# Two loads of a decode kernel cut into seven parts by partitions

## The chip, the cores and the metric

The kernel runs on one core of one Trainium2 chip. The metric is the device time of one execution in microseconds (us), the median of several runs. Five engines work side by side: PE multiplies matrices (PEld is its loading of weights), DVE and ACT work on vectors, POOL fills memory, and SP issues nearly all transfers. The transfers themselves are carried out by 16 DMA engines that the core has to itself. SBUF, the memory on the core, has 128 partitions; a load of a tile brings 128 rows from HBM, one for each partition.

## The reference

Two layers of a decode step, run twice with the same weights and caches. A layer is attention with one new token for each of 8 sequences over a cache of 4096 positions (32 query heads share 4 key and value heads), then a feed-forward network with a tanh GELU:

```python
x = x + _A_ref(_layernorm(x), A_k_cache, A_v_cache, A_wq, A_wo)
x = x + _B_ref(_layernorm(x), B_w1, B_b1, B_w2, B_b2)
x = x + _A_ref(_layernorm(x), A_k_cache, A_v_cache, A_wq, A_wo)
x = x + _B_ref(_layernorm(x), B_w1, B_b1, B_w2, B_b2)
```

with

```python
q = (x @ wq).reshape(B, Sq, Hq, Dh).transpose(0, 2, 1, 3)
p = softmax(einsum("bhqd,bhkd->bhqk", q, k) * Dh ** -0.5)
o = einsum("bhqk,bhkd->bhqd", p, v)          # then @ wo
h = gelu(x @ w1 + b1)                        # then @ w2 + b2
```

x is 8 x 1024, wq and wo are 1024 x 4096 and 4096 x 1024, w1 and w2 are 1024 x 3584 and 3584 x 1024, each cache is 8 x 4 x 4096 x 128, all in float32. Every weight and every cache is read from HBM, most of it twice, and each byte is used in one or two matmuls.

## The kernel before

All large data go through one tile, `arena` (line 58): 128 partitions of 218 units of 256 float32 (1 KB a partition). A place in it is a first unit and a number of units; 8 units (8 KB a partition, 1 MB in all) hold one piece of a cache. Three regions A, Bb and C start at units 0, 64 and 128, and a ring of four slots at 184.

`stream` (line 155) is the list of all loads in the order in which they are wanted, each with its place. `pump` (lines 158 to 163) issues from its head on SP's queue as long as the head's place is free, and `give` (line 71) frees a place behind its last use and calls `pump`. So the order of the loads is that of `stream`, and the time of an issue is set by the work that frees its place. Each issue waits on semaphores for that work, and also for the load eight places ahead of it in the queue, since eight semaphores are used in turn.

The order in `stream`: wq, then for each of the 8 sequences its K and V; K 7 and V 7, those of the last sequence, come in smaller loads, V 7 as four of 32, 16, 8 and 8 units (line 467). Then wo, w1, w2 and again wq, in loads of 8 units through the ring (lines 470 to 473). The second layer goes through the sequences backwards, and what is still in SBUF of the last two is not loaded again. At its end stand wo in two loads, w1 in two of 56 units (line 481, one for each half of the hidden units), and w2 in six of 40 to 4 units (line 482).

`values` (line 365) multiplies a piece of V with the probabilities, `expand` (line 172) a normalised row with wq or w1, and `project` (line 267) with wo or w2. `expand` goes through the loads of a half in turn (`loads`, line 165), frees them as they are used, and starts on a load when it has landed whole. Both loads of the change are read by PE alone.

The profile names w1 and w2 alike, `in_B_w_dram`, and a row of it that names L162 is an issue in `pump`.

Of the kernel before, what the change touches and what calls it, by code (L numbers as in the profile page):

```python
# [14 lines left out]
P = 128  # L15
B, D = 8, 1024
# [18 lines left out]
KB = 256  # L35
# [11 lines left out]
def decode_layers(ctx: ExitStack, tc: tile.TileContext, x, kc, vc, wq, wo, w1, b1, w2, b2, out):  # L47


    nc = tc.nc  # L50
# [7 lines left out]
    arena = const.tile([P, N_KB * KB], F32, name="arena")  # L58
# [5 lines left out]
    def is_free(at, n):  # L64
        return not any(u in used for u in range(at, at + n))

    def take(at, n, who):
        assert is_free(at, n), (who, at, n)
        used.update(dict.fromkeys(range(at, at + n), who))

    def give(at, n):
        for u in range(at, at + n):
            used.pop(u)
        pump()
# [79 lines left out]

    stream = []
    held = {}

    def pump():
        while stream and is_free(stream[0][1], stream[0][2]):
            key, at, n, src = stream.pop(0)  # L160
            take(at, n, key)
            nc.sync.dma_start(out=arena[:, at * KB:at * KB + src.shape[1]], in_=src)  # L162
            held[key] = at, n

    def loads(name):
# [137 lines left out]
    def v_keys(b):  # L303
        return [("v", b, r // NH, r % NH) for r in range(NR)]
# [124 lines left out]
    def weights(name, dram, parts, kept=0):  # L429

        for u in range(dram.shape[0]):
            a = 0
            end = dram.shape[2] - (kept if u == 1 else 0)
            for i, (at, n) in enumerate(parts[u]):
                cols = min(n * KB, end - a)
                stream.append((((name, u) if dram.shape[0] > 1 else name, i), at, n, dram[u, :, a:a + cols]))
                a += cols
            assert a == end
# [13 lines left out]
    A, C, Bb = AT_A, AT_C, AT_B  # L452
# [25 lines left out]
        cache(1, k_keys(b), kc[b], [(k_at, 8)])  # L478
        cache(1, v_keys(b), vc[b], [(v_at, 8)])
    weights("o1", wo, [[(C, SLOT), (A, SLOT)]])  # L480
    weights("i1", w1, [[(Bb, 56)], [(C, 56)]])
    weights("p1", w2, [[(A, 40), (A + 40, 28), (A + 68, 20), (A + 88, 12), (A + 100, 8), (A + 108, 4)]])

    kept = set(k_keys(7)) | set(v_keys(7)) | set(k_keys(6))
# [5 lines left out]
    open_queries()  # L490
    rsum = row_sums()
    pump()
    nc.vector.tensor_reduce(rsum, x_row, AX.X, ALU.add)  # L493
    nc.sync.dma_start(out=b2T, in_=b2)
# [111 lines left out]
```

## Time and profile before

| what | us |
|---|---|
| median of 3 runs | 871.89 (871.6 to 872.33) |
| the profiled execution | 871.66 |
| its span, first to last instruction | 869.9 |
| PE busy in it | 536.0 (62%) |
| DVE busy in it | 179.6 (21%) |
| ACT busy in it | 48.7 (6%) |

The span is what the trace covers; the 1.8 us that the execution has beyond it lie around it. The page gives busy times of each engine, the span in 40 slices, the DMA queues (q1 is SP's, q8 and q14 bring instructions, q10 is ACT's), the chain of work that ended last, and groups of instructions. In a row of the timeline the number in brackets is how long the engine sat idle before, and what ended that.

### The profile page before, as it was taken

What the parts mean: (1) busy time and instruction counts of PE and PEld (TensorE: products, weight loads), DVE (VectorE), ACT (ScalarE), POOL (GpSimd) and SP (SyncE); (2) the same over time, 40 slices, a digit from 0 to 9 for tenths busy, and PEclk for the clock granted to TensorE, in tenths of its full rate; (3) what the DMA queues carried; (4) which work ended last, traced back from release to release, by engine and by line L of the source; (5) the groups of instructions that cost most, each with busy time, mean ns of one, the idle gap of its engine ahead of it and who ended that gap; (6) DMA issues with size and microseconds to landing.
All of it is one profiled execution on the core that took longest, in us unless ns stands there. A gap on an engine that the chain in (4) does not pass through costs nothing.

```text
span 869.9 us, 9280 instructions
## 1 busy us (share of the span) xinstructions
PE 536.0 (62%) x4120; PEld 184.3 (21%) x4120; DVE 179.6 (21%) x601; ACT 48.7 (6%) x77; POOL 2.3 (0%) x13
## 2 busy tenths in 40 slices
PE   0546574655657576866666777876575555755565
PEld 0212121211212122222222122222121211222222
DVE  0001231313122232200110033332231313120011
ACT  0200000000000011000000010000000000000000
POOL 0000000000000000000000000000000000000000
PEclk9977787777777788777886798987777877778879
DMA  9999999999999999999999999999999999999997
GB/s 391 435 433 432 434 432 432 435 431 435 431 429 432 434 422 428 411 417 419 421 419 416 411 423 439 438 431 432 432 434 432 435 434 435 429 435 437 421 421 304
DMA packets 17608, 369.45 MB, mean 425 GB/s; under 512 B 2208, under 2 KB 2464, under 8 KB 4000
## 3 DMA queue, kind: packets, MB, share of 16 engines
q1 hardware_dynamic: 17424, 368.73, 99.2%
q8 instruction: 32, 0.52, 0.2%
q10 hardware_dynamic: 144, 0.13, 0.0%
q14 instruction: 8, 0.07, 0.0%
HBM read 368.72 MB, written 0.13 MB: 424 GB/s over the span
## 4 chain that ended last, share of the span: by engine, by line
DMA 75%; PE 21%; DVE 1%; another core or an unknown queue 1%; ACT 1%; issue 0%; SPq 0%; ACTq 0%; DVEq 0%
DMA arena<-in_A_v_cache_dram 28%; DMA arena<-in_A_k_cache_dram 20%; DMA arena<-in_B_w_dram 17%; PE o_ps L375 7%; PE sps L318 5%; DMA arena<-in_A_wo_dram 5%; PE acc L189 3%; DMA arena<-in_A_wq_dram 3%; DMA x_row<-in_A_x_dram 3%; PE y L283 2%; PE sps L390 1%; PE sps L353 1%; PE s_ps L318 1%; ACT arena L342 0%
## 5 line engine op out<-in xcount | busy, mean ns | idle before, releaser
L318 PE MATMUL sps<-arena 128*32 128x512 f32 x944 | 137.2, 719 | 118.4 <-DMA arena<-in_A_k_cache_dram 106.7
L375 PE MATMUL o_ps<-arena 128*32 128x512 f32 x1024 | 151.6, 732 | 10.2 <-DMA arena<-in_A_v_cache_dram 10.1
L283 PE MATMUL y<-arena,oT 128*32 128x256 f32 x960 | 79.1, 474 | 50.7 <-DMA arena<-in_A_wo_dram 31.2
L189 PE MATMUL acc<-arena,xnT 128*32 128x512 f32 (+3 forms) x640 | 78.2, 596 | 46.2 <-DMA arena<-in_B_w_dram 27.0
L318 PEld LDWEIGHTS sps<-arena 128*32 128x32 f32 x944 | 29.7, 125 | 192.9 <-DMA arena<-in_A_k_cache_dram 98.2
L383 DVE SCALAR_TENSOR_TENSOR scratch<-o_ps,misc,scratch 128x128 f32<-128x128 f32 x192 | 67.4, 351 | 6.8
L353 PE MATMUL sps<-ident,arena 128*128 128x128 f32 x128 | 31.1, 388 | 43.5 <-ACT arena L342 31.6
L283 PEld LDWEIGHTS y<-arena,oT 128*32 128x32 f32 x960 | 31.8, 129 | 94.5 <-DMA arena<-in_A_wo_dram 32.6
L375 PEld LDWEIGHTS o_ps<-arena 128*32 128x32 f32 x1024 | 33.0, 130 | 86.5 <-issue 73.8
L342 ACT ACTIVATE arena<-arena,bias 128x1024 f32<-128x1024 f32 x16 | 18.4, 1150 | 505.9 <-DVE scratch L339 505.9
L326 DVE TENSOR_SCALAR_CACHE_REDUCE arena<-sps 128x512 f32<-128x512 f32 x30 | 20.8, 692 | 124.9 <-PE sps L318 124.9
L392 DVE TENSOR_TENSOR oT<-sps,scratch 128x8 f32<-128x8 f32 x64 | 11.1, 173 | 154.4 <-PE sps L390 154.4
L189 PEld LDWEIGHTS acc<-arena,xnT 128*32 128x32 f32 x640 | 22.0, 124 | 91.4 <-DMA arena<-in_A_wq_dram 34.1
L390 PEld LDWEIGHTS sps<-misc,scratch 128*128 128x128 f32 x128 | 21.5, 211 | 63.8 <-DVE scratch L383 39.9
L381 DVE TENSOR_SCALAR scratch<-o_ps,misc 128x128 f32<-128x128 f32 x64 | 22.0, 344 | 54.7 <-PE o_ps L375 54.7
L353 PEld LDWEIGHTS sps<-ident,arena 128*128 128x128 f32 x128 | 19.7, 191 | 52.4 <-ACT arena L342 35.4
L390 PE MATMUL sps<-misc,scratch 128*128 128x8 f32 x128 | 27.4, 286 | 1.2 <-DVE scratch L383 1.2
L335 PE MATMUL sps<-scratch,misc 128*128 128x128 f32 x32 | 7.8, 326 | 18.9 <-DVE scratch L331 18.6
L295 DVE SCALAR_TENSOR_TENSOR x_row<-y,x_row 128x256 f32<-128x256 f32 x4 | 1.7, 425 | 85.0 <-PE y L283 85.0
L358 DVE COPY arena<-sps 128x512 f32<-128x512 f32 x16 | 11.1, 692 | 39.4 <-PE sps L353 39.4
L360 PE MATMUL sps<-scratch,misc 128*128 128x32 f32 x32 | 10.2, 411 | 12.5 <-DVE arena L358 12.5
L131 PE MATMUL sps<-nmean,rsum 128*128 128x64 f32 x8 | 2.1, 358 | 25.3 <-DVE rsum L493 23.6
(77 smaller groups left out, 143.2 us busy)
## 6 DMA issues: line engine op xcount, KB each, us to landing
arena<-in_B_w_dram SPq DMA_DIRECT2D x27, 1024.0 KB, 8.6
arena<-in_A_wo_dram SPq DMA_DIRECT2D x15, 1024.0 KB, 8.2
arena<-in_A_wq_dram SPq DMA_DIRECT2D x14, 1024.0 KB, 8.1
arena<-in_B_w_dram SPq DMA_DIRECT2D x2, 7168.0 KB, 45.3
arena<-in_A_k_cache_dram SPq DMA_DIRECT2D x3, 4096.0 KB, 18.2
arena<-in_A_v_cache_dram SPq DMA_DIRECT2D x3, 4096.0 KB, 24.5
arena<-in_A_v_cache_dram SPq DMA_DIRECT2D x4, 2048.0 KB, 12.0
arena<-in_A_wq_dram SPq DMA_DIRECT2D x1, 7680.0 KB, 39.9
```

The lines of the kernel that those rows point to most:

```text
L189: nc.tensor.matmul(acc[32 * j:32 * j + 32, r * P:(r + len(ts)) * P], xnT[:, kt * B:kt * B + 32], blocks[:, ts[0] - t0:ts[-1] - t0 + 1:4], ...
L283: nc.tensor.matmul(y[32 * j:32 * j + 32, 0:Q4], lhs[:, kt * B:kt * B + 32], arena[:, e:e + Q4], start=(kt == 0), stop=(kt == n_k - 1))
L318: nc.tensor.matmul(ps[32 * g:32 * g + 32, :], q[:, c:c + 32], kt[:, g * CH:(g + 1) * CH], start=(j == 0), stop=(j == HKV - 1))
L326: nc.vector.tensor_scalar(row[:, half * CH:(half + 1) * CH], ps, SCALE, None, op0=ALU.mult, op1=ALU.max, accum_out=st["mx"][:, half:half + 1])
L342: nc.scalar.activation(row, row, AF.Exp, bias=bias, scale=1.0, accum_out=ls)
L353: nc.tensor.transpose(pp[:, t * P:(t + 1) * P], row[:, c:c + P], ident)
L358: nc.vector.tensor_copy(s[:, half], src)
L375: nc.tensor.matmul(o[32 * g:32 * g + 32, :], s[:, g], v[:, g * CH:(g + 1) * CH], start=(half == 0), stop=(half == NH - 1))
L381: nc.vector.tensor_scalar(r, o[:, 0:P], sel_t[:, 0:1], None, op0=ALU.mult)
L383: nc.vector.scalar_tensor_tensor(r, o[:, t * P:(t + 1) * P], sel_t[:, t:t + 1], r, op0=ALU.mult, op1=ALU.add)
L390: nc.tensor.matmul(po[:, 0:REP], scratch[:, a:a + DH], sel_h, start=True, stop=True)
L392: nc.vector.tensor_tensor(oT_v[:, j * REP:(j + 1) * REP, b], po[:, 0:REP], scratch[:, a + j * REP:a + (j + 1) * REP], ALU.mult)
```

## The change

Two loads are picked out by their keys and kept in a set, `split`: the second of V 7 in the first layer (16 units, 2 MB, 16 KB a row) and a part of w1's second half in the second layer. For the latter the load of 56 units becomes one of 36 and one of 20 units (2.5 MB, 20 KB a row). `pump` issues a load of the set in seven parts by partitions, one behind the other on the same queue: partitions 0 to 111, then five times three partitions (112 to 126), then partition 127. Every byte still goes from the same place to the same place.

```diff
     stream = []
     held = {}
+    split = set()
+    uneven = [(0, 112)] + [(a, min(a + 3, P)) for a in range(112, P, 3)]
 
     def pump():
         while stream and is_free(stream[0][1], stream[0][2]):
             key, at, n, src = stream.pop(0)
             take(at, n, key)
-            nc.sync.dma_start(out=arena[:, at * KB:at * KB + src.shape[1]], in_=src)
+            dst = arena[:, at * KB:at * KB + src.shape[1]]
+            for a, b in uneven if key in split else ((0, P),):
+                nc.sync.dma_start(out=dst[a:b], in_=src[a:b])
             held[key] = at, n
...
-    weights("i1", w1, [[(Bb, 56)], [(C, 56)]])
+    weights("i1", w1, [[(Bb, 56)], [(C, 36), (C + 36, 20)]])
+    split.update(((0, v_keys(B - 1)[4]), (("i1", 1), 1)))
```

On SP's queue, this stood where the first layer's V 7 is loaded, followed by the first loads of wo (a row is an issue: line, target and source, partitions by float32 elements, and what it waits for; DMAHW0 to 7 are the eight semaphores of earlier loads):

```order
L162 DMA arena<-in_A_v_cache_dram 128x8192 [waits DMAHW4_49,PE_49]
L162 DMA arena<-in_A_v_cache_dram 128x4096 [waits PE_49]
L162 DMA arena<-in_A_v_cache_dram 128x2048 [waits PE_49]
L162 DMA arena<-in_A_v_cache_dram 128x2048 [waits DMAHW3_49,PE_49]
L162 DMA arena<-in_A_wo_dram 128x2048 [waits DMAHW5_49,Activation_49]
```

And this stands there now, on the same queue:

```order
L166 DMA arena<-in_A_v_cache_dram 128x8192 [waits DMAHW4_49,PE_49]
L166 DMA arena<-in_A_v_cache_dram 112x4096 [waits PE_49]
L166 DMA arena<-in_A_v_cache_dram 3x4096
L166 DMA arena<-in_A_v_cache_dram 3x4096 [waits DMAHW3_49]
L166 DMA arena<-in_A_v_cache_dram 3x4096 [waits DMAHW5_49]
L166 DMA arena<-in_A_v_cache_dram 3x4096 [waits DMAHW6_49]
L166 DMA arena<-in_A_v_cache_dram 1x4096 [waits DMAHW7_49]
L166 DMA arena<-in_A_v_cache_dram 128x2048 [waits DMAHW0_49,PE_49]
L166 DMA arena<-in_A_v_cache_dram 128x2048 [waits DMAHW1_49,PE_49]
L166 DMA arena<-in_A_wo_dram 128x2048 [waits DMAHW2_49,DVE_49]
```

The load of 128 rows of 4096 has become one of 112 rows, five of three (one of them, like the first, without a wait, is left out here) and one of a single row. The issues behind it now wait for the parts, since those stand eight places ahead of them.

On SP's queue, at the end of the second layer, this stood where w1's second half and w2 are loaded:

```order
L162 DMA arena<-in_A_wo_dram 128x16384 [waits DMAHW5_49,PE_49]
L162 DMA arena<-in_B_w_dram 128x14336 [waits DMAHW6_49,PE_49]
L162 DMA arena<-in_B_w_dram 128x14336 [waits DMAHW7_49,PE_49]
L162 DMA arena<-in_B_w_dram 128x10240 [waits DMAHW0_49,PE_49]
L162 DMA arena<-in_B_w_dram 128x7168 [waits DMAHW1_49,PE_49]
L162 DMA arena<-in_B_w_dram 128x5120 [waits PE_49]
```

And this stands there now:

```order
L166 DMA arena<-in_B_w_dram 128x14336 [waits DMAHW4_49,PE_49]
L166 DMA arena<-in_B_w_dram 128x9216 [waits DMAHW5_49,PE_49]
L166 DMA arena<-in_B_w_dram 112x5120 [waits PE_49]
L166 DMA arena<-in_B_w_dram 3x5120 x4
L166 DMA arena<-in_B_w_dram 3x5120 [waits DMAHW6_49]
L166 DMA arena<-in_B_w_dram 1x5120 [waits DMAHW7_49]
L166 DMA arena<-in_B_w_dram 128x10240 [waits DMAHW0_49,PE_49]
L166 DMA arena<-in_B_w_dram 128x7168 [waits DMAHW1_49,PE_49]
L166 DMA arena<-in_B_w_dram 128x5120 [waits DMAHW2_49,PE_49]
L166 DMA arena<-in_B_w_dram 128x3072 [waits DMAHW3_49,PE_49]
```

Where two loads of 14,336 elements a row stood there are now one of those, one of 9,216, and seven parts of 5,120; w2's first loads follow unchanged, but for what they wait for. On PE the order is the same; its matmuls on the two loads wait for the parts.

## The prediction

> **What bounds the kernel now.** I read the page first, its slices, its DMA counts and its chain.
>
> ```profile
> span 869.9 us, 9280 instructions
> ...
> DMA  9999999999999999999999999999999999999997
> GB/s 391 435 433 432 434 432 432 435 431 435 431 429 432 434 422 428 411 417 419 421 419 416 411 423 439 438 431 432 432 434 432 435 434 435 429 435 437 421 421 304
> DMA packets 17608, 369.45 MB, mean 425 GB/s; under 512 B 2208, under 2 KB 2464, under 8 KB 4000
> ...
> q1 hardware_dynamic: 17424, 368.73, 99.2%
> q8 instruction: 32, 0.52, 0.2%
> ...
> DMA 75%; PE 21%; DVE 1%; another core or an unknown queue 1%; ACT 1%; issue 0%; SPq 0%; ACTq 0%; DVEq 0%
> ```
>
> The 16 DMA engines are busy in every slice, and almost all of it is SP's queue, q1. Its count tells how a load is made: 121 issues (120 loads and the output) times 144 is 17,424, and 144 is 128 rows plus 16. So every load is one packet a row and one closing packet on each of 16 engines, eight rows an engine. A row is never cut between engines. PE's 21% of the chain is work that frees buffers ahead of need; the chain of waits in order of time ends on a transfer:
>
> ```profile
> 822.41 0.33 SPq L162
> 822.78 43.16 DMA arena<-in_B_w_dram
> 865.99 0.68 PE y L283 x8
> 866.70 0.42 DVE x_row L295
> ```
>
> The last piece of w2 lands at 865.99, and 3.9 us of fixed work follow. So the time is the time at which the last of the 16 engines delivers its last row. Windows over the middle show that no engine rests there (columns: window, length, five busy times, clock, DMA share, GB/s; a share can pass 1 since neighbouring packets overlap a little):
>
> ```profile
> 400.00:440.00 40.00, 23.97 (x261) 9.37 (x260) 5.85 (x21) 3.16 (x5) 0.00 (x0) 0.87 1.01 420
> ...
> 600.00:700.00 100.00, 57.81 (x367) 18.09 (x366) 25.47 (x84) 3.68 (x6) 0.00 (x0) 0.76 1.00 434
> ```
>
> An engine that falls behind therefore has no later pause in which to catch up; what the latest engine loses is carried to the end. The same view over the last microseconds shows how unequal the engines are:
>
> ```profile
> 861.50:862.00 0.50, 0.00 (x0) 0.00 (x0) 0.00 (x0) 0.00 (x0) 0.00 (x0) 1.00 0.88 361
> ...
> 862.50:862.75 0.25, 0.25 (x12) 0.16 (x8) 0.00 (x0) 0.00 (x0) 0.00 (x0) 1.00 0.48 197
> ...
> 863.50:864.00 0.50, 0.16 (x4) 0.00 (x0) 0.00 (x0) 0.00 (x0) 0.00 (x0) 1.00 0.49 197
> 864.00:864.50 0.50, 0.00 (x0) 0.00 (x0) 0.00 (x0) 0.00 (x0) 0.00 (x0) 1.00 0.49 197
> ...
> 865.00:865.25 0.25, 0.25 (x12) 0.17 (x8) 0.00 (x0) 0.00 (x0) 0.00 (x0) 1.00 0.21 82
> 865.25:865.50 0.25, 0.25 (x12) 0.08 (x4) 0.00 (x0) 0.00 (x0) 0.00 (x0) 1.00 0.05 16
> ```
>
> Half of the engines are through by 862.5, the other half by about 865.2: a lead of some 2.8 us. While eight work, they move 197 GB/s at a share of 0.49, 25 GB/s each, no more than the 26 GB/s each of 420 over 16. So what limits an engine is its own, or that of the place it writes to, and not a total that others could leave to it. One cause of the lead stands in the DMA view of the last stretch, 862 to 866:
>
> ```profile
> q8 instruction: 1, 0.02, 1.7%
> ```
>
> One fetch of 16 KB of instructions took 1.7% of 16 engines for 4 us, 1.09 us. The page has 32 of them, 35 us; on eight engines alone that is 4.4 us each. I take 4.4 us as the whole lead of the unburdened half (2.8 us is what was left of it at the end).
>
> **The price of a row.** w2's 20-unit piece has rows of 20 KB, like the second split load. PE's waits for it and for the piece before it give its time:
>
> ```profile
> 852.34 1.93 PE L283 MATMUL y<-arena,oT 128*32 128x256 f32 x32 [1.65 <-DMA arena<-in_B_w_dram]
> ...
> 858.45 2.37 PE L283 MATMUL y<-arena,oT 128*32 128x256 f32 x40 [1.26 <-DMA arena<-in_B_w_dram]
> ```
>
> 858.45 less 852.34 is 6.11 us for eight rows an engine, 0.764 us a row. A row of 16 KB, as in the V 7 load, is 16/20 of it, 0.611 us.
>
> **What the change does, part by part.**
>
> *The 112 rows.* Seven rows an engine in place of eight: each engine is spared 0.611 us at V 7 and 0.764 us at w1, 1.37 us together, if the seven rows run as the eight did.
>
> *The 16 rows.* They go as loads of three rows. One row is one packet and one packet is one engine's, so such a load can use three engines at most, and the other thirteen wait for none of it. The five loads and the single row then put six rows on one engine and five on two, if they are always the same three. What a load of three costs has no row in this trace; it lies between two ends:
> - its rows run side by side, one row time a load. The fullest engine has 7 + 6 = 13 rows for 8: five more, 5 × (0.611 + 0.764) = 6.9 us.
> - its rows run one after another, three row times a load, because three neighbouring partitions are one place and the 25 GB/s belong to the place. Then 16 row times follow the seven: 23 for 8, fifteen more, 15 × (0.611 + 0.764) = 20.6 us.
>
> The windows at the end leave open whether the rate is the engine's or the place's, since each engine keeps to its own eight rows there. I take the upper end: an eighth of a tile, 16 rows, takes eight row times in every load of this trace, so the lower end's five to six are a speed that it never shows; and the three rows of one load are the closest neighbours that there are. Off that come the 4.4 us, if the three engines belong to the half with the lead. I take it that they do: 20.6 − 4.4 = **+16.2 us**. If they do not, it is +20.6 us.
>
> [...]
>
> [...]
>
> *The cut of w1 into 36 and 20 units.* One more load, issued from a queue that is ahead. PE can begin on the first part at about 825 and not at 831.62:
>
> ```profile
> 814.76 3.66 PE L189 MATMUL acc<-arena,xnT 128*32 128x512 f32 x22 [6.65 <-DMA arena<-in_B_w_dram]
> ...
> 831.62 1.07 PE L189 MATMUL acc<-arena,xnT 128*32 128x512 f32 x4 [8.41 <-DMA arena<-in_B_w_dram]
> ```
>
> (814.76 plus 36/56 of the 16.86 us between the two starts is 825.6.) It gains nothing, for PE then waits for w2 anyway (the two rows at 852 and 858 show waits of 1.65 and 1.26 us); what hides it is the transfer, and without that cover it would be a gain of a few us of PE work.
>
> *SP's issues and waits.* Thirteen more issues at 0.33 us (the row at 822.41) are 4.3 us of an SP that waits for most of the span:
>
> ```profile
> SPq L162 <- PE sps L390: 168.7, 21, 19.1
> SPq L162 <- DMA arena<-in_A_v_cache_dram: 121.4, 13, 29.0
> ```
>
> Nothing. Each piece waits for the load eight places ahead of it in the queue, and behind a waiting piece stand the rest of V 7 and the first wo loads at the one place, all of w2 at the other. Before the change w2's last issue comes 43 us ahead of its landing (822.78 to 865.99), so a wait of a few us does not empty an engine's queue. After slow pieces it could: the wo loads wait for the pieces of V 7 one by one. I leave that in the upper end.
>
> *PE at V 7.* It is busy, not waiting, when these rows come:
>
> ```profile
> 347.58 6.43 PE L375 MATMUL o_ps<-arena 128*32 128x512 f32 x32
> ...
> 358.61 1.07 PE L283 MATMUL y<-arena,oT 128*32 128x256 f32 x16
> ```
>
> So lateness of a few us costs PE nothing there; of more than that, PE frees the wo slots late, which falls into the time in which the three engines are late already.
>
> **The sum.** It is made on the profiled run, 871.66 us (span 869.9 and 1.8 around it; the median of the runs is 871.89): 871.66 + 16.2 = 887.9 us.
>
> **The rivals.**
> 1. *One after another, on engines without a lead:* + 20.6, 892.3 us. Half of the engines have no lead, and one such among the three is enough; against it, the halves may well be blocks.
> 2. *Side by side, on engines without a lead:* +6.9, 878.6 us. For it: the trace shows no engine hindered by another.
> 3. *Side by side, on engines with the lead; not slower.* The thirteen end 1.37 us sooner, at 870.3 us. The fullest engine ends at 6.9 − 4.4 = +2.5, 874.2 us; the two with five rows more than seven at 4 × 1.375 − 4.4 = +1.1, 872.8 us. It decides from the lead: at 6.9 us the sum is nought, and beyond it the change gains, by 1.37 us at most. A fetch takes more from its engine than its own 1.09 us if it also holds up the rows beside it; a quarter more makes the lead 5.5 us and the time 873.1 us. I take 871 to 874 us.
> 4. *It does not do what it says:* the pieces go to ever other engines, each has 7 + 1 rows, and the time stays at 871.7 to 872 us.
>
> **How the numbers follow.** One after another: 0.52 (with a lead 0.35, without 0.17). Side by side without a lead 0.17, with it 0.25. Evenly spread 0.06. The forecast is the likeliest, 887.9 us. Cases of both "slower" and "no change" hold much, so the range runs from the third rival's lower side, 871.2 us, to just over the first, 892.5 us; the likeliest alone would be 884 to 892.5 us. Within 0.2% (1.7 us, about what a measurement of this kernel can tell from no change, so 870.1 to 873.6 us) fall the fourth and two thirds of the third: 0.22. A gain of over 0.2% would need more than the 1.37 us that the thirteen engines are spared, so only 0.03 is kept for it. Slower has the rest, 0.75.
>
> **What would show it.** On the page, q1 with 17,600 packets. A split load has 112 + 16, five times 3 + 3, and 1 + 1 packets, 160 in all: 16 more than before at V 7, and 160 more at w1, whose other part keeps 144. Any other count refutes that three rows mean three engines. In windows at the end, a long tail with a share near 3/16 = 0.19 shows three late engines, 10 us or more for one after another, 1 to 3 us for side by side; a staircase like before's shows rivals 3 or 4. At V 7, lateness of the first wo loads by several us shows the first half of the sum, and the same lateness again at w2 the second. The forecast fails if three neighbouring rows move at 0.611 us a row together.

## The result

The change makes the kernel slower: 894.33 us (median of 6 runs, 893.84 to 894.75) against 871.78 us for the kernel before (median of 6, 871.56 to 874.25), a ratio of 1.0253 with a 95% interval of 1.0240 to 1.0267. That is 22.5 us. The forecast was 887.9 us, and its range ended at 892.5 us.

The page of the changed kernel (its span, slices and DMA counts; the profiled execution took 894.75 us):

```profile
span 893.0 us, 9313 instructions
...
DMA  9999999999999999999999999999999999999996
GB/s 409 442 421 421 430 449 429 423 437 432 438 423 435 432 418 274 401 417 421 421 419 417 423 434 432 438 437 427 432 434 430 438 435 426 433 433 421 222 384 258
DMA packets 17784, 369.45 MB, mean 414 GB/s; under 512 B 2256, under 2 KB 2512, under 8 KB 4048
...
q1 hardware_dynamic: 17600, 368.73, 98.9%
```

The DMA engines are as busy as before and carry the same 369.45 MB, but two slices of the GB/s row stand out: 274 in the sixteenth, where V 7 is loaded (428 before), and 222 in the thirty-eighth, where w1's second half is (421 before). The windows of the changed kernel over V 7 and over w1 (window, length, five busy times, clock, DMA share, GB/s):

```profile
340.00:345.00 5.00, 1.95 (x7) 1.25 (x7) 1.01 (x5) 1.93 (x4) 0.00 (x0) 0.50 0.98 295
345.00:350.00 5.00, 3.01 (x14) 1.57 (x18) 1.05 (x2) 0.40 (x1) 0.00 (x0) 0.50 1.00 221
350.00:355.00 5.00, 5.00 (x30) 1.18 (x22) 1.40 (x4) 0.00 (x0) 0.00 (x0) 0.63 0.96 175
355.00:360.00 5.00, 1.04 (x10) 0.36 (x13) 1.48 (x5) 0.00 (x0) 0.00 (x0) 0.71 0.76 213
360.00:365.00 5.00, 5.00 (x34) 1.30 (x26) 1.48 (x5) 0.00 (x0) 0.00 (x0) 0.61 1.01 426
830.00:835.00 5.00, 2.55 (x22) 0.64 (x14) 0.87 (x2) 0.00 (x0) 0.00 (x0) 1.00 0.99 207
835.00:840.00 5.00, 0.00 (x0) 0.00 (x0) 0.00 (x0) 0.00 (x0) 0.00 (x0) 0.50 0.89 179
840.00:845.00 5.00, 4.68 (x20) 1.61 (x20) 0.00 (x0) 0.00 (x0) 0.00 (x0) 0.50 0.99 172
```

and of the kernel before, over the same stretch of V 7:

```profile
345.00:350.00 5.00, 4.10 (x18) 1.82 (x22) 1.05 (x2) 0.55 (x2) 0.00 (x0) 0.50 0.98 411
350.00:355.00 5.00, 5.00 (x34) 1.37 (x30) 2.00 (x7) 0.00 (x0) 0.00 (x0) 0.67 1.01 421
```

A share of 1.00 at 221 GB/s is the main reading of this case: nearly all 16 engines have a packet under way, and each packet takes about twice as long. The trace also holds each packet's own time, which says the same. From 345 to 350 us a row of 16 KB takes 1.18 us (mean of 62), where before it took 0.615 us (mean of 72). Rows of loads that the change does not touch slow down too: from 845 to 850 us a row of 40 KB of w2 takes 3.5 us (mean of 17), where before it took 1.52 us. A few late engines would show a small share instead (three of 16 would be 0.19). So most of the loss is no tail. The last microseconds of the changed kernel show how little tail there is:

```profile
884.00:885.00 1.00, 0.17 (x4) 0.00 (x0) 0.00 (x0) 0.00 (x0) 0.00 (x0) 1.00 0.44 180
885.00:886.00 1.00, 0.54 (x12) 0.37 (x16) 0.00 (x0) 0.00 (x0) 0.00 (x0) 1.00 0.17 70
886.00:887.00 1.00, 0.96 (x20) 0.30 (x12) 0.00 (x0) 0.00 (x0) 0.00 (x0) 1.00 0.09 37
887.00:888.00 1.00, 0.06 (x4) 0.06 (x8) 0.00 (x0) 0.00 (x0) 0.00 (x0) 1.00 0.06 25
```

Where PE waits for a load, its start marks the landing. In the timeline of the changed kernel these are w1's first half, the 36 units and, at the end, w2's last load:

```profile
822.79 4.48 PE L193 MATMUL acc<-arena,xnT 128*32 128x512 f32 x22 [5.34 <-DMA arena<-in_B_w_dram]
840.32 3.63 PE L193 MATMUL acc<-arena,xnT 128*32 128x512 f32 x16 [7.78 <-DMA arena<-in_B_w_dram]
...
889.19 0.64 PE L287 MATMUL y<-arena,oT 128*32 128x256 f32 x8 [0.18 <-DMA arena<-in_B_w_dram]
```

Before, the first and the last of these stood at 814.76 and 865.99. So V 7's cut has made the stream 8.0 us late, and w1's another 15.2 us (23.2 at the end). The second row is the odd one: the 36 units are an ordinary load that stands ahead of the cut one, and were due at 833.6 (the prediction's 825.6 and the 8.0 of V 7); they land 6.7 us later than that. (In run e2_columns, below, where the same 36 units stand in a stream that is not slowed, they land 10.89 us after w1's first half, at 827.06 and 816.17 us; the prediction's 825.6 and 814.76 are 10.84 apart.)

### The profile page after: what moved, and what is told of

It reads as the page before. It is cut to its first block, busy times and chain, and to the rows that moved or that the text cites. A ratio compares the mean times of both kernels' runs of the same rounds, so it can differ in the third digit from the quotient of the medians.

```text
span 893.0 us, 9313 instructions
## 1 busy us (share of the span) xinstructions
PE 544.1 (61%) x4124; PEld 186.5 (21%) x4124; DVE 179.5 (20%) x601; ACT 48.6 (5%) x77; POOL 2.3 (0%) x13
## 2 busy tenths in 40 slices
DMA packets 17784, 369.45 MB, mean 414 GB/s; under 512 B 2256, under 2 KB 2512, under 8 KB 4048
## 3 DMA queue, kind: packets, MB, share of 16 engines
q1 hardware_dynamic: 17600, 368.73, 98.9%
## 4 chain that ended last, share of the span: by engine, by line
DMA 75%; PE 20%; another core or an unknown queue 2%; DVE 1%; ACT 1%; issue 0%; SPq 0%; ACTq 0%; DVEq 0%
DMA arena<-in_A_v_cache_dram 28%; DMA arena<-in_A_k_cache_dram 16%; DMA arena<-in_B_w_dram 15%; DMA arena<-in_A_wo_dram 9%; PE o_ps L379 8%; PE sps L322 5%; DMA arena<-in_A_wq_dram 4%; DMA x_row<-in_A_x_dram 3%; PE acc L193 2%; PE y L287 2%; PE sps L394 1%; PE s_ps L322 0%; PE sps L357 0%; DVE arena L330 0%
## 5 line engine op out<-in xcount | busy, mean ns | idle before, releaser
L379 PE MATMUL o_ps<-arena 128*32 128x512 f32 x1024 | 154.2, 743 | 14.8 <-DMA arena<-in_A_v_cache_dram 14.8
L193 PE MATMUL acc<-arena,xnT 128*32 128x512 f32 (+3 forms) x644 | 82.1, 613 | 51.5 <-DMA arena<-in_B_w_dram 32.6
L346 ACT ACTIVATE arena<-arena,bias 128x1024 f32<-128x1024 f32 x16 | 18.4, 1148 | 504.6 <-DVE scratch L343 504.6
L362 DVE COPY arena<-sps 128x512 f32<-128x512 f32 x16 | 11.1, 692 | 39.8 <-PE sps L357 39.8
L218 DVE TENSOR_SCALAR scratch<-acc,rs 128x512 f32<-128x512 f32 (+1 forms) x8 | 5.5, 684 | 65.8 <-PE acc L193 65.8
## 6 DMA issues: line engine op xcount, KB each, us to landing
arena<-in_A_k_cache_dram SPq DMA_DIRECT2D x3, 4096.0 KB, 19.3
```

The lines of the kernel that those rows point to most:

```text
L193: nc.tensor.matmul(acc[32 * j:32 * j + 32, r * P:(r + len(ts)) * P], xnT[:, kt * B:kt * B + 32], blocks[:, ts[0] - t0:ts[-1] - t0 + 1:4], ...
L346: nc.scalar.activation(row, row, AF.Exp, bias=bias, scale=1.0, accum_out=ls)
L362: nc.vector.tensor_copy(s[:, half], src)
L379: nc.tensor.matmul(o[32 * g:32 * g + 32, :], s[:, g], v[:, g * CH:(g + 1) * CH], start=(half == 0), stop=(half == NH - 1))
```

## The experiments

Each diff is against the changed kernel. Differences are between medians. The kernel before was run again beside them: e1 to e4 are measured against its 872.31 us (13 runs), e5 to e9 against its 872.57 us (6 runs). The two loads that are cut are called V 7 and w1 for short. Three ideas were to be told apart first. *Place*: the partitions fall into groups, called places here, and each place takes data at a limited rate; an ordinary load of 128 rows gives each engine a place of its own, and a load that doesn't is slow throughout. *Overload*: the forecast's idea, three engines have more rows than the others. *Number*: each further load costs a wait.

### No engine has more rows than another

**Run e1_two**: 112 rows and one load of 16, by its packets (below) on 16 engines, so that each has eight rows again.

```diff
-    uneven = [(0, 112)] + [(a, min(a + 3, P)) for a in range(112, P, 3)]
+    uneven = [(0, 112), (112, P)]
```

> Both loads as 112 rows and one load of 16 rows: every engine moves eight rows again, and no small loads are left. Theory place (the rate belongs to the place that is written, and a load whose engines do not each have a place of their own is slow): the 112 rows stay as slow as in the changed kernel, about 1.2 us a row at V 7 for 0.61 and 1.5 to 2 us at w1 for 0.76, and the 16 rows crowd into few places; 10 to 16 us over before, 882 to 888 us. Theory overload (three engines have 13 rows for 8): no engine is overloaded, within 1 us of before, 871 to 873 us. Theory number (each further load costs a wait on the queue): three loads more, not 13, so under a quarter of the loss, 872 to 877 us.

Measured: 890.71 us, +18.4 (ratio 1.0219, 1.0203 to 1.0235). q1 has 17,600 packets again, as it must if each of the two parts of a load closes on 16 engines. Without any uneven count, 18 of the 22.5 us are there, more even than the 10 to 16 that *place* gave. Overload is not the main cause. The windows of this run have the same mark:

```profile
345.00:350.00 5.00, 1.99 (x10) 0.90 (x14) 0.70 (x2) 0.00 (x0) 0.00 (x0) 0.50 1.05 233
350.00:355.00 5.00, 5.00 (x28) 0.98 (x20) 1.40 (x4) 0.00 (x0) 0.00 (x0) 0.54 0.93 182
```

**Run e2_columns**: seven parts too, but by columns, each of all 128 rows (w1's load is cut into 36 and 20 units as in the change).

```diff
-    uneven = [(0, 112)] + [(a, min(a + 3, P)) for a in range(112, P, 3)]
...
-            for a, b in uneven if key in split else ((0, P),):
-                nc.sync.dma_start(out=dst[a:b], in_=src[a:b])
+            w = src.shape[1]
+            cuts = [w * i // 7 // 64 * 64 for i in range(7)] + [w] if key in split else [0, w]
+            for a, b in zip(cuts, cuts[1:]):
+                nc.sync.dma_start(out=dst[:, a:b], in_=src[:, a:b])
```

> The same two loads in seven parts each, but by columns: all 128 rows in each part. Theory place and theory overload: each engine keeps its eight rows and its places, 871 to 874 us (84 more row packets an engine set cost next to nothing). Theory number: as slow as the changed kernel, 885 to 895 us.

Measured: 873.16 us, +0.85 (ratio 1.0008, 0.9999 to 1.0018), though q1 has 19,296 packets here, 1,872 more than before. The number of loads, SP's further issues and waits, and the cut of w1 cost nothing that this measurement can tell.

**Runs e3_halves and e4_middle**: two parts of 64 rows; and rows 32 to 95 as one part, with rows 0 to 31 and 96 to 127 as two more.

```diff
-    uneven = [(0, 112)] + [(a, min(a + 3, P)) for a in range(112, P, 3)]
+    uneven = [(0, 64), (64, P)]
```

```diff
-    uneven = [(0, 112)] + [(a, min(a + 3, P)) for a in range(112, P, 3)]
+    uneven = [(32, 96), (0, 32), (96, P)]
```

> Both loads as partitions 0 to 63 and 64 to 127. Every engine moves four rows of each, two engines to a place if there are 16 places of eight partitions. Theory place: all eight rows at double time, 8 x (0.611 + 0.764) = 11 us over before, 880 to 886 us. Theory overload: equal loads, 871 to 873 us. Theory number: two or three loads more, 872 to 877 us.

> Both loads as partitions 32 to 95, 0 to 31 and 96 to 127. By the map of places that theory place takes, the 64 in the middle have a place for each engine and run at full speed, and only the two outer parts share, two engines to a place: 4 x (0.611 + 0.764) = 5.5 us at most over before, 873 to 879 us, clearly below the two halves. Theory overload: 871 to 873 us. Theory number: one load more than the two halves each time, so slower than these. If any cut by partitions were slow, whatever the places, this would be as slow as the halves or slower.

Measured: 890.73 us, +18.4 (1.0211, 1.0195 to 1.0226), and 882.52 us, +10.2 (1.0130, 1.0111 to 1.0150). Which 64 rows go together decides (18.4 against 10.2 us), as *place* has it; both lie 3.5 to 5 us above its figures, so something is missing in it.

### Each of the two cuts alone, and the 112 rows alone

**Runs e5_v7 and e6_w1** make one of the two cuts each.

```diff
-    weights("i1", w1, [[(Bb, 56)], [(C, 36), (C + 36, 20)]])
-    split.update(((0, v_keys(B - 1)[4]), (("i1", 1), 1)))
+    weights("i1", w1, [[(Bb, 56)], [(C, 56)]])
+    split.add((0, v_keys(B - 1)[4]))
```

```diff
-    split.update(((0, v_keys(B - 1)[4]), (("i1", 1), 1)))
+    split.add((("i1", 1), 1))
```

> Only the load of V 7 is cut, w1's second half stays one load of 56 units. In the trace of the change the last load of V 7 lands 8.1 us later than before, and the end comes another 15 us later after the cut load of w1. Lateness is carried through (the streams stay full in between): 871.8 + 8 = 879 to 882 us. If slack in between takes it up, or if the lateness at w1 is what counts: 872 to 875 us.

> Only the part of w1 is cut. Lateness adds: 885 to 888 us (871.8 + 15). If the second cut is costly only because the first one has thrown the engines out of step: 879 to 882 us.

Measured: 880.32 us, +7.75 (1.0097, 1.0065 to 1.0130), and 885.26 us, +12.7 (1.0149, 1.0127 to 1.0171). Lateness is carried from V 7 to the end, some 500 us later. The 12.7 us of w1's cut alone are 2.5 us less than the 15.2 that it adds in the trace of the change; but the interval of the 12.7 runs from 11.1 to 14.9 us, so this difference is not clear of the noise.

**Run e9_only112** brings 112 rows of each of the two loads and leaves out the other 16; the matmuls work on what stood there before.

```diff
-    uneven = [(0, 112)] + [(a, min(a + 3, P)) for a in range(112, P, 3)]
+    uneven = [(0, 112)]
```

> Both loads bring 112 rows only; the other 16 rows are left out (the matmuls work on what stood there before). Theory of the prediction (seven rows run as the eight did): 1.37 us less, 870 to 871 us. Theory place (a load whose engines do not each have a place of their own is slow throughout and holds up the loads beside it): 880 to 887 us, most of the 18.4 us that 112 and 16 rows cost.

Measured: 886.67 us, +14.1 (1.0164, 1.0147 to 1.0182). This is the run that decides: an eighth less to bring in both loads, and 14 us more. Its PE rows for w1's first half, the 36 units and, at the end, w2's last load:

```profile
822.51 4.46 PE L193 MATMUL acc<-arena,xnT 128*32 128x512 f32 x22 [5.86 <-DMA arena<-in_B_w_dram]
837.11 3.56 PE L193 MATMUL acc<-arena,xnT 128*32 128x512 f32 x16 [5.36 <-DMA arena<-in_B_w_dram]
...
881.73 0.64 PE L287 MATMUL y<-arena,oT 128*32 128x256 f32 x8 [0.18 <-DMA arena<-in_B_w_dram]
```

At w1's first half it is 7.75 us late, hardly less than the change (8.0). So by these two traces the small loads cost next to nothing at V 7 on top of the 112 rows. At the end it is 15.7 us late, 8.0 more, where the change adds 15.2: at w1 the small loads cost 7.2 us. No run has the small loads without the 112 rows, so this is what they cost on top of them. The ordinary 36 units ahead of the 112 rows land at 837.11, 3.8 us beyond 825.6 + 7.75. They are complete only when the slowest engine has its rows, and by then the engines ahead of it are already in the 112 rows. The packets of this run show it: a row of the 36 units takes 1.37 us from 820 to 825 us, before the first of the 112 rows starts at 829.2 us, and 2.63 us (mean of the last eight) from 830 to 835 us, beside them.

**Run e8_apart**: the rows of each load of three lie five partitions apart.

```diff
-    uneven = [(0, 112)] + [(a, min(a + 3, P)) for a in range(112, P, 3)]
...
-            for a, b in uneven if key in split else ((0, P),):
-                nc.sync.dma_start(out=dst[a:b], in_=src[a:b])
+            if key in split:
+                nc.sync.dma_start(out=dst[0:112], in_=src[0:112])
+                for a in range(112, 117):
+                    nc.sync.dma_start(out=dst[a:a + 11:5], in_=src[a:a + 11:5])
+                nc.sync.dma_start(out=dst[127:P], in_=src[127:P])
+            else:
+                nc.sync.dma_start(out=dst, in_=src)
```

> As the change (894.3 us), but the three rows of each small load lie five partitions apart, so that they are no neighbours; the engines get the same numbers of rows. Theory place, as the prediction has it (neighbouring rows go one after another): the tail of the small loads gets shorter, at both places by a half or more; at most the 4 us that the change lies above the same cut with one load of 16 rows, so 889 to 892 us. If neighbours do not hinder each other and the three engines' six rows each are the tail: 893 to 896 us.

Measured: 894.13 us, +21.6 (1.0248, 1.0232 to 1.0264), no different from the change. In the whole kernel, that the three rows are neighbours costs nothing that this measurement can tell.

### Loads by themselves

Four kernels leave out the computation and only load rows of 16 KB. A DVE copy waits for each group of loads before the next is issued, so the idle time ahead of the copy is the group's. Each group ran three times; in the rows below the idle time is that of all three. For example, two groups of the first of these kernels and one of the third:

```python
        dma(out=p1[0:112], in_=s1[0:112])
        done(flag, ends)
...
        dma(out=p0, in_=s0)
        dma(out=p1[0:112], in_=s1[0:112])
        dma(out=p2, in_=s2)
        done(flag, ends)
...
        load(0), small(6, 4, 5), load(2)
        done(flag, ends)
```

**Run m1_shapes**: shapes alone, and shapes between two loads of 128 rows.

> Leaves out all of the computation: it only loads 16 KB rows of V 7 in several shapes, each group behind the landing of the group before, three times over; a DVE copy waits for each group, so its idle time is the group's. One row of 16 KB takes 0.611 us on an engine with nothing in its way; c is the fixed time of any group. Theory place (engines that write to one place share its speed): lone loads of rows 0-127 c + 4.9 us, 32-95 c + 2.4, 0-63 c + 4.9, 0-111 between c + 4.3 and c + 8.6 and clearly over c + 4.9, 112-127 c + 2.4, three neighbours c + 1.8, three rows five apart and a single row c + 0.6. Theory interplay (a load of 112 rows by itself runs at full speed, and becomes slow only among loads of engines that are out of step): 0-111 c + 4.3 alone, and slow only in the groups of three loads with a lead. In groups of three loads with the shape in the middle: 128 rows c + 14.7; 112 rows c + 14.1 if the seven rows run as the eight do, c + 17 to 18 if each takes twice as long; halves c + 19.6 if they only share places, and more than that if they hold up the loads beside them; with a load of eight rows ahead, which puts eight engines one row behind, more again if being out of step is what costs. Six small loads in the middle instead of 128 rows: c + 9.8 + 3.7 if the three rows of a load run side by side, c + 9.8 + 9.8 if one after another.

The groups of its DVE, by line: L64 is 128 rows alone, L66 rows 0 to 111, L68 rows 0 to 63, L70 rows 32 to 95, L78 three neighbouring rows, L80 three rows five apart; L86, L90, L95, L99 have 128 rows, 112 rows, two halves and rows 32 to 95 between two loads of 128; L104 has the seven parts of the change there, L109 its six small loads.

```profile
L109 DVE COPY flag<-arena 128x4 f32<-128x4 f32 x3 | 0.5, 171 | 67.1 <-DMA arena<-in_A_v_cache_dram 67.1
L68 DVE COPY flag<-arena 128x4 f32<-128x4 f32 x3 | 0.5, 171 | 23.6 <-DMA arena<-in_A_v_cache_dram 23.6
...
L95 DVE COPY flag<-arena 128x4 f32<-128x4 f32 x3 | 0.5, 171 | 67.5 <-DMA arena<-in_A_v_cache_dram 67.5
...
L70 DVE COPY flag<-arena 128x4 f32<-128x4 f32 x3 | 0.5, 170 | 15.6 <-DMA arena<-in_A_v_cache_dram 15.6
...
L78 DVE COPY flag<-arena 128x4 f32<-128x4 f32 x3 | 0.5, 170 | 9.7 <-DMA arena<-in_A_v_cache_dram 9.7
L80 DVE COPY flag<-arena 128x4 f32<-128x4 f32 x3 | 0.5, 170 | 9.2 <-DMA arena<-in_A_v_cache_dram 9.2
L90 DVE COPY flag<-arena 128x4 f32<-128x4 f32 x3 | 0.5, 170 | 57.9 <-DMA arena<-in_A_v_cache_dram 57.9
L99 DVE COPY flag<-arena 128x4 f32<-128x4 f32 x3 | 0.5, 170 | 44.2 <-DMA arena<-in_A_v_cache_dram 44.2
L104 DVE COPY flag<-arena 128x4 f32<-128x4 f32 x3 | 0.5, 170 | 88.0 <-DMA arena<-in_A_v_cache_dram 88.0
...
L66 DVE COPY flag<-arena 128x4 f32<-128x4 f32 x3 | 0.5, 170 | 26.8 <-DMA arena<-in_A_v_cache_dram 26.8
...
L64 DVE COPY flag<-arena 128x4 f32<-128x4 f32 x3 | 0.5, 170 | 21.7 <-DMA arena<-in_A_v_cache_dram 21.7
L86 DVE COPY flag<-arena 128x4 f32<-128x4 f32 x3 | 0.5, 170 | 51.2 <-DMA arena<-in_A_v_cache_dram 51.2
```

Divided by three: 128 rows alone take 7.2 us, 112 rows 8.9, rows 0 to 63 7.9, rows 32 to 95 5.2. The load of 112 rows is slow by itself; *interplay* as its only cause is out. The packets of the first of the three turns agree: over 0.9 us for one row, where 0.61 is the usual, take 18 of 128 rows, 74 of 112, 59 of rows 0 to 63 and 11 of rows 32 to 95. Three neighbouring rows take 3.2 us and three rows five apart 3.1: here *place* was wrong, which had the neighbours 1.2 us slower. Between two loads of 128 rows, 128 rows give 17.1 us, 112 rows 19.3 (+2.2, where seven rows at full speed would save 0.6), the halves 22.5, rows 32 to 95 14.7, and the seven parts 29.3, +12.2. The six small loads give 22.4: beside the 12.2 us of two loads with nothing between them (next run) +10.2, close to the 9.8 of "one after another".

But +2.2 us for 112 rows, and 20/16 of it at w1, are 5 us, not the 14.1 of the whole kernel; and the small loads, most of the 12.2 here, are the lesser part there.

**Run m2_step**: the same with loads of eight rows ahead, which are to put eight engines one or more rows behind the others (out of step, for short), and single rows.

> Leaves out all of the computation, as the kernel of load shapes did: groups of loads of 16 KB rows, each behind the landing of the one before, three times over. Two loads of 128 rows with 128 rows between them took 17.1 us there, with 112 rows 19.3. Here 0, 2, 4 or 6 loads of eight rows (0, 4, ... 28) go ahead, one row each for eight engines, which are then 0 to 3.7 us behind the others. Theory step (while the engines ahead are in the load of 112 rows, those behind take about twice as long for ordinary rows): 112 rows cost 2 us more than 128 without lateness, and about the lateness on top, so some 2, 3, 4.5 and 6 us. Theory of a price of the load alone: 2 us at every lateness. Then six loads of a single row between two loads of 128, all of row 0, of row 127 or of row 64. Theory place (a row costs the others something only where its engine writes to another engine's place): row 0 adds 6 row times, 3.7 us, and leaves the others at their speed; rows 64 and 127 add more than that. If any engine that falls behind slows all: the three agree. Six small loads of the change behind one load of 128 rows, with nothing behind them: if their three rows go one after another whatever runs beside, 9.8 us more than that load; if side by side, 3.7; with 128 rows behind, 22.4 us in all were measured before.

L80, L84, L92 have 128 rows in the middle at a lateness of 0, 2 and 6 rows; L82, L86, L94 have 112 rows there, and L96 the halves at 6; L98 has nothing in the middle, L100 six times row 0, L102 six times row 127; L110 is the six small loads behind one load of 128.

```profile
L98 DVE COPY flag<-arena 128x10 f32<-128x10 f32 x3 | 0.5, 174 | 36.6 <-DMA arena<-in_A_v_cache_dram 36.6
L100 DVE COPY flag<-arena 128x10 f32<-128x10 f32 x3 | 0.5, 174 | 48.6 <-DMA arena<-in_A_v_cache_dram 48.6
L80 DVE COPY flag<-arena 128x10 f32<-128x10 f32 x3 | 0.5, 173 | 51.4 <-DMA arena<-in_A_v_cache_dram 51.4
L82 DVE COPY flag<-arena 128x10 f32<-128x10 f32 x3 | 0.5, 173 | 57.8 <-DMA arena<-in_A_v_cache_dram 57.8
L84 DVE COPY flag<-arena 128x10 f32<-128x10 f32 x3 | 0.5, 173 | 62.9 <-DMA arena<-in_A_v_cache_dram 62.9
L86 DVE COPY flag<-arena 128x10 f32<-128x10 f32 x3 | 0.5, 173 | 82.2 <-DMA arena<-in_A_v_cache_dram 82.2
L102 DVE COPY flag<-arena 128x10 f32<-128x10 f32 x3 | 0.5, 173 | 57.7 <-DMA arena<-in_A_v_cache_dram 57.7
L110 DVE COPY flag<-arena 128x10 f32<-128x10 f32 x3 | 0.5, 173 | 41.3 <-DMA arena<-in_A_v_cache_dram 41.3
...
L92 DVE COPY flag<-arena 128x10 f32<-128x10 f32 x3 | 0.5, 173 | 71.6 <-DMA arena<-in_A_v_cache_dram 71.6
L94 DVE COPY flag<-arena 128x10 f32<-128x10 f32 x3 | 0.5, 173 | 84.9 <-DMA arena<-in_A_v_cache_dram 84.9
L96 DVE COPY flag<-arena 128x10 f32<-128x10 f32 x3 | 0.5, 173 | 103.0 <-DMA arena<-in_A_v_cache_dram 103.0
```

112 rows cost 2.1 us with engines in step (57.8 − 51.4, over three), and 6.4, 5.6 and 4.4 us behind 2, 4 and 6 loads of eight rows. These make eight engines as many rows late if they use the same eight each time, which the trace does not show. Two or more of them double or triple the price, which *step* had right in kind; that it grows with the lateness was wrong. One did not raise it: behind a load of eight rows, m1_shapes has 18.7 us for 128 rows and 20.5 for 112, +1.8. (The groups of 128 rows become longer too, by 3.8 us at a lateness of two rows, more than the two row times.) At w1's 20 KB the same would be 20/16 of it, so both loads together 10 to 14.5 us, as an estimate from 4.4 and 6.4 us: the 14.1 of the whole kernel is at the upper side of that. How far out of step the engines are at V 7 and at w1 was not measured; at the end of the kernel before, half of them are some 2.8 us behind. The halves go from 5.4 us to 10.5.

Six single rows on one engine add 4.0 us if they are row 0, about their own six row times, and 7.0 if they are row 127. The count and the bytes are the same; only the partition differs. That it is the same engine each time is not shown directly, since the trace does not name a packet's engine; that six rows cost about six row times says that one engine has all six. The small loads behind one load of 128 take 13.8 us, 6.5 more than the load alone, between the two values expected; the rest, some 4 us, is what they cost the load behind them.

**Run m3_map**: the last test for other rows.

> Leaves out all of the computation: six loads of a single row (each on the same engine) between two loads of 128 rows of 16 KB, for fourteen choices of the row, three times over; a group with nothing between took 12.2 us, with row 0 16.2, with row 127 or 64 19.2 to 19.3. Theory place: the engine's own place in an ordinary load is a few partitions; rows of these cost 4 us and all others 7. From the full speed of rows 32 to 95 and the half speed of rows 0 to 63 as one load, rows 32 places apart share a place: rows 0, 1, 3, 32 and 35 cost 4 us; 4, 8, 16, 31, 36, 63, 64, 96 and 124 cost 7. If the first eight rows are the engine's own: 0, 1, 3, 4 cost 4 us, 8 and 32 cost 7. If row 0 is cheap because it is the engine's first row, or for another reason: 1, 3 and 32 cost 7.

Rows 32 and 36 stand at L87 and L91:

```profile
L91 DVE COPY flag<-arena 128x10 f32<-128x10 f32 x3 | 0.5, 174 | 57.4 <-DMA arena<-in_A_v_cache_dram 57.4
...
L87 DVE COPY flag<-arena 128x10 f32<-128x10 f32 x3 | 0.5, 173 | 48.8 <-DMA arena<-in_A_v_cache_dram 48.8
```

With 36.5 us for nothing between, row 32 costs 4.1 us a group and row 36 7.0. All fourteen fell as *place* said: rows 0, 1, 3, 32, 35 cost 4.0 to 4.1 us; 4, 8, 16, 31, 36, 63, 64, 96, 124 cost 6.9 to 7.2. So the own place of the engine that brings a single row fits partitions 0 to 3 and 32 to 35 (2, 33 and 34 were not tried).

**Run m4_three**: the small loads at several places.

> Leaves out all of the computation: between two loads of 128 rows of 16 KB (12.2 us with nothing between) the change's six small loads (10.5 us more were measured) and variants of them that put the same numbers of rows on the same three engines: at these engines' own places (rows 0, 4, 8), at the places of three other engines, one each (rows 64, 68, 72), all at one other engine's place (rows 112 to 114), and five rows apart as in the whole kernel. Theory place: own places 3.7 to 4.1 us more; one foreign place each 7 us more, as one engine at a foreign place cost; all three at one foreign place the most, 10 us or more, since four engines share it then, and the five apart between 7 and 10.5. If the number of engines behind the others is what costs, and not where they write: all variants near 10.5. Last, the same 16 rows as four loads of four rows that lie four apart, one for each of four engines, each at a place of its own but a foreign one: four rows on four engines, 7 us more or less by the same theory.

L75 has nothing between, L77 the change's small loads, L79 rows 0, 4 and 8, which *place* takes for the engines' own places, L81 rows 64, 68 and 72, for it three foreign places (places of other engines), L83 rows 112 to 114, for it one foreign place, L85 five rows apart, L87 four loads of four rows.

```profile
L77 DVE COPY flag<-arena 128x10 f32<-128x10 f32 x3 | 0.5, 174 | 68.4 <-DMA arena<-in_A_v_cache_dram 68.4
L79 DVE COPY flag<-arena 128x10 f32<-128x10 f32 x3 | 0.5, 174 | 48.9 <-DMA arena<-in_A_v_cache_dram 48.9
L81 DVE COPY flag<-arena 128x10 f32<-128x10 f32 x3 | 0.5, 174 | 57.5 <-DMA arena<-in_A_v_cache_dram 57.5
L85 DVE COPY flag<-arena 128x10 f32<-128x10 f32 x3 | 0.5, 173 | 57.4 <-DMA arena<-in_A_v_cache_dram 57.4
...
L83 DVE COPY flag<-arena 128x10 f32<-128x10 f32 x3 | 0.5, 173 | 76.6 <-DMA arena<-in_A_v_cache_dram 76.6
```

Against the 36.6 us of three groups with nothing between, the own places of *place* cost 4.1 us a group, a foreign one for each 7.0, all at one 13.3, the change's loads 10.6. The five apart cost 6.9 and the loads of four 5.0. The last lies below the 7 expected. With the same number and size of rows in loads of the same form, it is the partitions that set the price (4.1 to 13.3 us); that what counts is how many engines write to one place at a time is how *place* reads it, since no run shows the engines. In every run here row r of the source goes to partition r, so the runs cannot tell a place in SBUF from one in HBM; no run sends rows to other partitions.

## Why the prediction was wrong

*What bounds the kernel.* Right. What is lost at V 7, where the same bytes move at about half the rate for nearly 20 us, appears, undiminished, at the end (8.0 us late at w1's first half in the change; +7.75 us in all with V 7 alone cut, e5_v7).

*The 112 rows.* This is the step that failed: "each engine is spared 0.611 us at V 7 and 0.764 us at w1, 1.37 us together, if the seven rows run as the eight did". They don't. The load of 112 rows is slow throughout, its rows taking about twice as long (rows of 16 KB 1.18 us for 0.615 in the change), and it slows what is still under way of the load ahead (rows of the 36 units 2.63 us for 1.37, e9_only112). It cost 14.1 us (12.8 to 15.9, e9_only112) instead of sparing 1.37, an error of 15.5 us. It is the choice of partitions that costs and not the number of loads (e2_columns +0.85 us, and e3_halves +18.4 beside e4_middle +10.2). That a load of 112 rows takes the engines out of their own places is the reason that fits these runs and the single rows; which rows an engine has in it is not shown, and the size of the loss is not derived from it. The condition was named and given no price. The prediction itself suspected that the rate may belong to the place, and then used that for the three neighbouring rows alone.

*The 16 rows.* 16 row times (22.0 us) less the lead (4.4) made 17.6 us; in the whole kernel they cost 22.5 − 14.1 = 8.4. This error of 9.2 us in the other direction hides more than half of the first: 887.9 + 15.5 − 9.2 = 894.2. That the forecast came as near as 6.4 us is therefore luck. No run shows that the three engines have the lead, or which engines they are. Between two loads by themselves the upper end was right in size (10.2 to 10.6 us at V 7's row size, 9.8 by the forecast), but only in part for the reason given, neighbours at one place: five partitions apart the rows still cost 6.9 us, so being neighbours makes 3.7 of it, and with nothing behind them the small loads cost 6.5. In the whole kernel it isn't the neighbours (894.13 us in e8_apart, 894.33 in the change). That the small loads cost next to nothing at V 7 and 7.2 us at w1 fits a lead that is there once and then used up; that was not tested by itself.

*The cut of w1, SP's issues and waits.* Right at nothing (e2_columns). The emptying of queues that was left in the upper end has little room at V 7: the share of 0.76 in the window from 355 leaves 0.24 of 5 us, 1.2 us, late engines included.

*PE at V 7.* Right that it is the loads that count: from 355 to 360 PE is busy for 1.04 us and otherwise waits for them.

*The rivals.* All four took a 112-row load at full speed for granted, so none could reach 894 us. At half its speed the seven rows would have been fourteen row times for eight, 6 × 1.375 = +8.3 us in place of −1.37; a rival with that price would have stood at 897.5 us. The packets do not settle the fourth, evenly spread pieces: they say that a load of three uses three engines, not that these are always the same. The single rows speak against it: six loads of row 0 cost 4.0 us, about six row times of 0.611, which six different engines would not need.

*The signs.* 17,600 packets came, so a load of three has three closing packets and by them uses three engines. Lateness at V 7 and again at w2 came. The long tail at a share of 0.19 did not: the windows show 0.17 for one microsecond and less from then on, as the sign had it for rows side by side (1 to 3 us). By this sign three late engines are not the main cost.

## What to carry to other kernels

Cut a large load by columns and keep all 128 partitions in each part: seven parts cost nothing measurable that way (+0.85 us, a ratio of 1.0008). Every cut of both loads by partitions that was tried here cost 10 to 22.5 us, and even the untouched loads beside it slowed down; a smaller load can take longer than the whole (112 rows 8.9 us, 128 rows 7.2). In a profile the mark of it is a DMA share near 1 at half the GB/s (1.00 at 221, where 0.98 and 411 stood before); too few busy engines show a small share (0.49 at the end of the kernel before, with half of them through).

## What was not expected of the hardware

Rows 0 to 63 by themselves took 7.9 us and all 128 rows 7.2; rows 32 to 95 took 5.2 (m1_shapes). The two sets of 64 rows differ about as *place* had it (by 2.7 us, for 2.5 by its figures); that 64 rows can take longer than 128 it does not explain.

Why 112 rows in step cost only 2.1 us and behind loads of eight rows up to 6.4, and why ordinary rows on all engines slow down beside a cut load, is not settled: shared places fit the single rows (4.0 to 4.1 us against 6.9 to 7.2) and the order of the two sets of 64 rows, but not that nearly every row is slow. With the 112 rows alone (e9_only112) five windows of 5 us over the two loads show 197 to 233 GB/s, about half of 421, as if every engine shared its place with another; the 175 of the change stands in a window that has its small loads too.
